# Batch 0's tails of k and v: issued by ScalarE ahead of its first table load instead of by GpSimd

## The chip, the cores and the metric

The kernel runs on one core of a Trainium2 chip. The metric is device time in microseconds (us) of one execution. Before the change the median of 3 runs is 270.94 us (270.31 to 272.93). The core's engines are TensorE (PE, with PEld for its weight loads), VectorE (DVE), ScalarE (ACT), GpSimd (POOL) and SyncE (SP). Each runs its own list of instructions in order, and issuing a DMA is one instruction of such a list.

## The reference

Two stages follow each other: an attention without softmax, and a feed-forward layer with a leaky ReLU.

```python
# q, k, v: (8 batches, 8 heads, 576 positions, 64)
def phi(x, c, s):
    r = np.maximum(x, 0.0)
    return np.concatenate([r * c, r * s], axis=-1)   # c, s: cos and sin of pi/2 * pos / 576
q_p, k_p = phi(q, cos_w, sin_w), phi(k, cos_w, sin_w)
kv  = np.einsum('bhsf,bhsd->bhfd', k_p, v)
z   = np.sum(k_p, axis=2)
num = np.einsum('bhsf,bhfd->bhsd', q_p, kv)
den = np.einsum('bhsf,bhf->bhs', q_p, z)[..., None] + 1e-06
attn = num / den                                     # -> x: (4608, 512)
h = x @ w_in                                         # (512, 2048)
out = np.maximum(0.01 * h, h) @ w_out                # (2048, 512)
```

## The kernel before

**Tiling.** The 576 positions of a batch are cut into a main part of 512 (four groups `j` of 128 partitions) and a tail of 64. Per batch, k and v give the 128x65 matrices `kv` of each head (64 columns of v and one of ones, which gives the denominator); q, scaled by cosine and sine and transposed, is multiplied with `kv` and divided into `xs` or `xp`; those rows, transposed again, are the right side of the first feed-forward product (`ps_h`, L460, L496, L782), whose leaky ReLU `g` enters the second (`ps_o`, L476, L883). Batches follow each other, and the tails of all q make a ninth group at the end. From batch 2 on a table of positions (`PLACE`, `AT`) sets the order; batches 0 and 1, which the change touches, are written out by hand, and the order is that of the code.

**The start, engine by engine.** SP issues, one behind the other, the two halves (heads 0 to 3, heads 4 to 7) of batch 0's q, then k's and v's first halves, k's and v's second halves (`load_main`, L93), and the eight pieces of the first weights (`load_w1`, L140). DVE clears a tile `blank`, with which TensorE runs 28 matmuls into an unused bank (`idle`, L168) until q is there. GpSimd makes the identity and the positions `pos` (L183 to L202), and then issues the four tail DMAs (`load_kvtail`, L103: k's tail and v's tail, each in two DMAs of 64 partitions by 4 heads by 64 numbers, so 256 bytes in one piece). ScalarE loads a table for the sine (L164), makes `cos_t` and `sin_t` (L216, L217) out of `pos`, and loads the table for ReLU and leaky ReLU (L218). Nothing of q, k or v can be scaled before `cos_t` and `sin_t` are made.

**Then batch 0.** DVE and ScalarE share the 16 scalings of q (`q_part`: half the heads, one group `j`, cosine or sine; groups 0 and 2 and the cosine of 3 are DVE's, group 1 and the sine of 3 are ScalarE's). TensorE transposes group by group (L366, `ps_qt`); each group needs both halves of the heads. ScalarE and DVE copy the results out (L247, L249). Then k's tail (`kpt`, DVE), k's first half (`kpm`), v's tail (`vtail`) and v's first half (`vmain`) are scaled or cast, behind 28 more blank matmuls (`kv_half(0, 0, "t", 14)`) TensorE makes the first half of `kv` (L290, L299, `ps_kvh`), and ScalarE casts it (L323). The second half of k follows on DVE and ScalarE, the second half of v is cast by GpSimd (L249). TensorE makes the numerators of the first half (L417, `ps_numh`), the second half of `kv`, the transposes `ps_xth` (L434) and the numerators of the second half, and goes over into the feed-forward layer of batch 0 (L460).

**DMA counters.** The DMAs that SP or ScalarE issues share eight completion counters in turn (`DMAHW0` to `DMAHW7`), and a ninth DMA waits until the first that used its counter has landed. GpSimd's have counters of their own (`DMASW`).

Of the kernel before, what the change touches and what calls it, by code (L numbers as in the profile page):

```python
# [18 lines left out]
def kernel(  # L19
# [14 lines left out]
    nc = tc.nc  # L34
# [49 lines left out]
    def staged(shape, name, soon=False):  # L84
        p, tag = (early, "early") if soon else (stage, "stage")
        return p.tile(shape, dt.float32, name=name, tag=tag)

    def load_main(nm, src, b, parts=(0, 1), soon=False):

        if parts[0] == 0:  # L90
            st[nm, b] = staged([P, H, J, D], f"{nm}st", soon)
        lo, hi = 4 * parts[0], 4 * parts[-1] + 4
        nc.sync.dma_start(  # L93
            st[nm, b][:, lo:hi],
            src[b, lo:hi, 0:MAIN, :].rearrange("h (p j) d -> p h j d", j=J),
        )

    def load_kvtail(nm, src, b, eng=nc.sync):

        t = kvtail.tile([P, H // 2, D], dt.float32, name=f"{nm}tl", tag="kvtail")  # L100
        v4 = src[b, :, MAIN:S, :].rearrange("(c o) p d -> o p c d", o=2)
        for o in range(2):
            eng.dma_start(t[o:P:2], v4[o])  # L103
        st[nm + "t", b] = t
# [41 lines left out]

    load_main("q", q, 0, (0,))
    load_main("q", q, 0, (1,))
    load_main("k", k, 0, (0,))
    load_main("v", v, 0, (0,))  # L150
    load_main("k", k, 0, (1,))
# [55 lines left out]
        allow_small_or_imprecise_dtypes=True,  # L207
    )
    sub_ = pos[:, J + 1 : J + 2]
    load_kvtail("k", k, 0, nc.gpsimd)  # L210
    load_kvtail("v", v, 0, nc.gpsimd)
    nc.vector.tensor_tensor(out=sub_, in0=sub_, in1=odd[:, 1:2], op=ALU.subtract)
    nc.vector.tensor_scalar(out=sub_, in0=sub_, scalar1=0.5, scalar2=None, op0=ALU.mult)
    cos_t = const.tile([P, J + 2], dt.float32, name="cos_t")
# [1189 lines left out]
```

## Time and profile before

| | |
|---|---|
| median of 3 runs | 270.94 us (270.31 to 272.93) |
| the profiled execution | 271.15 us, of which its span is 269.2 us |
| PE busy | 263.1 us, 98% of the span |
| DVE, ACT, POOL busy | 215.8, 203.9, 13.1 us |
| chain that ended last | PE 89%, DMA 5%, DVE 2% |
| tails of batch 0 | 4 DMAs of 64 KB, issued by POOL from 1.81 us to 4.42 us; 6.2 to 6.6 us to landing |

A row of the timeline or of the chain begins with its start and its length in us; the timeline's brackets hold the idle time of the engine before the row, and what ended it. Times in the text count from the start of the span.

### The profile page before, as it was taken

To read this page: it belongs to the slowest core of one execution; us is meant where nothing else is said; L and a number is where in the kernel's file an instruction comes from. 1 tells how busy PE (TensorE), PEld (TensorE's weight loads), DVE (VectorE), ACT (ScalarE), POOL (GpSimd) and SP (SyncE) were. 2 spreads that over 40 slices of the span, in tenths; PEclk is the share of its full clock that TensorE was granted. 3 is DMA by queue.
4 is the path that set the end of the run, shared out by engine and by line. 5 is a ranking of instruction groups with operands and counts; after the bars stand their busy time and mean duration, and the time that the engine had idled before them with its cause. 6 is when DMAs were issued, how large, how long until landed. Compare 5 with 4: busy or idle time off the path is not lost.

```text
span 269.2 us, 6819 instructions
## 1 busy us (share of the span) xinstructions
PE 263.1 (98%) x2742; PEld 230.1 (85%) x2742; DVE 215.8 (80%) x486; ACT 203.9 (76%) x347; POOL 13.1 (5%) x25
## 2 busy tenths in 40 slices
PE   8989999999999999999999999999999999999994
PEld 6976465666899989999999999999999999999983
DVE  5785798698997898897979797979789968966453
ACT  8756556695989998997798799888968757787621
POOL 5057001000000000000000000000000000000000
PEclk9999999999999999999999999999999999999999
DMA  6999999979999969999999799987267232200314
GB/s 221 380 394 413 394 367 376 366 140 285 285 248 285 193 206 245 360 168 256 270 238 140 247 280 185 173 243 162 65 102 178 45 74 67 111 2 0 156 41 117
DMA packets 86190, 57.05 MB, mean 212 GB/s; under 512 B 55632, under 2 KB 81232, under 8 KB 85648
## 3 DMA queue, kind: packets, MB, share of 16 engines
q1 hardware_dynamic: 85584, 55.98, 79.3%
q8 instruction: 21, 0.34, 0.5%
q10 hardware_dynamic: 448, 0.39, 0.4%
q0 software_dynamic: 128, 0.26, 0.3%
q14 instruction: 9, 0.07, 0.1%
HBM read 36.70 MB, written 9.44 MB: 171 GB/s over the span
## 4 chain that ended last, share of the span: by engine, by line
PE 89%; DMA 5%; DVE 2%; SPq 1%; issue 1%; POOL 0%; ACT 0%; DVEq 0%
PE ps_h L782 31%; PE ps_o L883 30%; PE ps_h L460 5%; PE ps_o L476 5%; PE ps_h L496 5%; DMA vst<-in_v_dram 4%; PE ps_num L381 3%; PE ps_h L883 3%; PE ps_o L973 2%; PE ps_kv L290 2%; DMA xT<-xs 1%; SPq L93 1%; PE ps_qt L366 1%; PE ps_numh L417 1%; PE ps_kvh L290 1%; PE ps_kv L299 1%
## 5 line engine op out<-in xcount | busy, mean ns | idle before, releaser
L883 PEld LDWEIGHTS <-g 128*128 128x128 f16 x584 | 56.3, 98 | 5.3
L782 PE MATMUL ps_h<-xT,w 128*128 128x256 f16 x336 | 49.0, 273 | 0.0
L782 PEld LDWEIGHTS <-w 128*128 128x128 f16 x448 | 47.9, 113 | 1.1 <-issue 0.2
L252 DVE TENSOR_TENSOR u<-ps_h,u 128x512 f32<-128x512 f32 x56 | 38.3, 685 | 10.2 <-PE ps_h L782 10.0
L883 PE MATMUL ps_o<-w,g 128*128 128x256 f16 x288 | 41.4, 273 | 0.0
L782 PEld LDWEIGHTS <-wa 128*128 128x128 f16 x336 | 36.0, 113 | 1.0 <-issue 0.4
L795 ACT ACTIVATE g<-ps_h 128x512 f16<-128x512 f32 x56 | 33.9, 605 | 3.7 <-PE ps_h L782 3.5
L802 ACT COPY u<-ps_h 128x512 f32<-128x512 f32 x56 | 32.7, 584 | 4.9 <-PE ps_h L782 4.8
L809 ACT ACTIVATE g<-u 128x1024 f16<-128x1024 f32 x28 | 29.7, 1062 | 8.4 <-DVE u L252 8.2
L782 PE MATMUL ps_h<-xw,wa 128*128 128x256 f16 x224 | 33.6, 273 | 0.0
L883 PE MATMUL ps_o<-wb,g 128*128 128x256 f16 x232 | 32.2, 273 | 0.0
L883 PEld LDWEIGHTS <-gs 128*128 128x128 f16 x256 | 24.9, 98 | 2.4
L901 ACT COPY ob<-ps_o 128x512 f32<-128x512 f32 (+1 forms) x32 | 18.1, 564 | 9.4 <-PE ps_o L883 9.1
L397 DVE TENSOR_TENSOR xs<-ps_num,rden 128x512 f16<-128x512 f32 x28 | 19.4, 691 | 1.0
L883 PE MATMUL ps_o<-w,gs 128*128 128x256 f16 x120 | 17.5, 273 | 0.0
L792 ACT COPY ps_h<-ps_h 128x512 f32<-128x512 f32 x28 | 16.0, 573 | 1.6 <-PE ps_h L782 0.7
L255 DVE TENSOR_TENSOR gs<-g 128x1024 f16<-128x1024 f16 x16 | 11.0, 685 | 7.8 <-ACT g L809 7.6
L782 PE MATMUL ps_h<-xT,wa 128*128 128x256 f16 x112 | 16.8, 273 | 0.2 <-DVE u L252 0.2
L883 PE MATMUL ps_o<-wb,gs 128*128 128x256 f16 x120 | 16.9, 273 | 0.0
L782 PE MATMUL ps_h<-xw,w 128*128 128x256 f16 x112 | 16.8, 273 | 0.0
L252 DVE TENSOR_TENSOR ob<-ps_o,ob 128x512 f32<-128x512 f32 (+1 forms) x22 | 14.7, 670 | 1.3 <-ACT ob L901 0.9
L496 PE MATMUL ps_h<-xT,w 128*128 128x512 f16 (+1 forms) x72 | 15.1, 355 | 0.0
(128 smaller groups left out, 435.6 us busy)
## 6 DMA issues: line engine op xcount, KB each, us to landing
qst<-in_q_dram SPq DMA_DIRECT2D x7, 1024.0 KB, 6.6
out_dram<-ob SPq DMA_DIRECT2D x14, 512.0 KB, 2.9
kst<-in_k_dram SPq DMA_DIRECT2D x6, 1024.0 KB, 7.9
vst<-in_v_dram SPq DMA_DIRECT2D x6, 1024.0 KB, 7.0
w1st<-in_moe_w_in_dram SPq DMA_DIRECT2D x8, 512.0 KB, 10.0
w2st<-in_moe_w_out_dram SPq DMA_DIRECT2D x4, 1024.0 KB, 12.3
kst<-in_k_dram SPq DMA_DIRECT2D x4, 512.0 KB, 8.4
vst<-in_v_dram SPq DMA_DIRECT2D x4, 512.0 KB, 8.9
```

What stands on the lines that cost most here:

```text
L252: nc.vector.tensor_tensor(out=o, in0=a, in1=b, op=ALU.add)
L397: nc.vector.tensor_tensor(out=xs, in0=ps[:, :, 0 : 4 * NE].rearrange("p a (b e) -> p a b e", e=NE)[:, :, :, 0:D], in1=rden.rearrange("p (a ...
L460: nc.tensor.matmul(ps[:, m % 2, lo:hi], lhsT=w1[m // 4][c // 2][:, c % 2, m % 4 : 512 : 4], rhs=xT[:, c, lo:hi], start=(c == 0 and lo == 0 ...
L476: nc.tensor.matmul(ps, lhsT=st["g", g][:, m, tt * P : (tt + 1) * P], rhs=w2[:, m, :], start=(m == 0), stop=(m == NFT - 1),)
L496: nc.tensor.matmul(ps[:, lo:hi], lhsT=w1[m // 4][c // 2][:, c % 2, m % 4 : 512 : 4], rhs=st["xT", g][:, c, lo:hi], start=(c == 0 and lo == 0),
L782: nc.tensor.matmul(bank[:, p], lhsT=w(c), rhs=st["xb", g][n][:, c], start=(fresh and p == 0 and c == 0), stop=(c == 1), skip_group_check=True,
L792: nc.scalar.copy(bank1[bj], bank1[bi])
L795: nc.scalar.activation(st["g" + nm, g][:, 2 * t : 2 * t + 2], bank1[bi], AF.Lrelu)
L802: nc.scalar.copy(st["u", g, t][:, n], bank1[bi])
L809: nc.scalar.activation(st["gt", g][:, :, 1, 2 * t : 2 * t + 2], st["u", g, t], AF.Lrelu)
L883: nc.tensor.matmul(bank[..., lo:hi], lhsT=st[G2[n], g][:, m, pair * P : (pair + 1) * P], rhs=W2[n](m)[:, lo:hi], start=(fresh and m == 0), ...
L901: nc.scalar.copy(o_at(g, half_, col, pair), bank_of(bi, pair, pair is None))
```

## The change

The two calls that load the tails of batch 0's k and v move up in the code, behind the two loads of q, and are given ScalarE as the issuing engine.

```diff
@@ -146,6 +146,8 @@
 
     load_main("q", q, 0, (0,))
     load_main("q", q, 0, (1,))
+    load_kvtail("k", k, 0, nc.scalar)
+    load_kvtail("v", v, 0, nc.scalar)
     load_main("k", k, 0, (0,))
     load_main("v", v, 0, (0,))
     load_main("k", k, 0, (1,))
@@ -207,8 +209,6 @@
         allow_small_or_imprecise_dtypes=True,
     )
     sub_ = pos[:, J + 1 : J + 2]
-    load_kvtail("k", k, 0, nc.gpsimd)
-    load_kvtail("v", v, 0, nc.gpsimd)
     nc.vector.tensor_tensor(out=sub_, in0=sub_, in1=odd[:, 1:2], op=ALU.subtract)
     nc.vector.tensor_scalar(out=sub_, in0=sub_, scalar1=0.5, scalar2=None, op0=ALU.mult)
     cos_t = const.tile([P, J + 2], dt.float32, name="cos_t")
```

The function that they call is the same:

```python
def load_kvtail(nm, src, b, eng=nc.sync):
    t = kvtail.tile([P, H // 2, D], dt.float32, name=f"{nm}tl", tag="kvtail")
    v4 = src[b, :, MAIN:S, :].rearrange("(c o) p d -> o p c d", o=2)
    for o in range(2):
        eng.dma_start(t[o:P:2], v4[o])
    st[nm + "t", b] = t
```

On ScalarE, at the very start of the program, this stands now (- before, + after; `ktl` and `vtl` are the tails, `warm` and `zero` one column each, whose only use is to have the table loaded):

```order
 L1399 UNCONDITIONAL_BRANCH
-L164 ACT_TABLE_LOAD
-L164 ACTIVATE warm<-zero 128x1
+L103 DMA ktl<-in_k_dram 64x4x64 x2
+L103 DMA vtl<-in_v_dram 64x4x64 x2
+L166 ACT_TABLE_LOAD
+L166 ACTIVATE warm<-zero 128x1
 L216 ACTIVATE cos_t<-pos,half_pi 128x6
 L217 ACTIVATE sin_t<-pos,zero 128x6
```

Four DMA issues stand ahead of the table load; the rest of ScalarE's list, and the lists of PE and DVE, keep their order. GpSimd's list is the same without its four issues.

On SP, at the start of its list, the DMAs are the same in the same order, with other waits. Before:

```order
L93 DMA qst_111<-in_q_dram 128x4x256 x2
L93 DMA kst_114<-in_k_dram 128x4x256
L93 DMA vst_116<-in_v_dram 128x4x256
L93 DMA kst_114<-in_k_dram 128x4x256
L93 DMA vst_116<-in_v_dram 128x4x256
L140 DMA w1st_120<-in_moe_w_in_dram 128x2x512 x2
```

After:

```order
L93 DMA qst_111<-in_q_dram 128x4x256 x2
L93 DMA kst_120<-in_k_dram 128x4x256
L93 DMA vst_122<-in_v_dram 128x4x256
L93 DMA kst_120<-in_k_dram 128x4x256 [waits DMAHW0_49]
L93 DMA vst_122<-in_v_dram 128x4x256 [waits DMAHW1_49]
L140 DMA w1st_126<-in_moe_w_in_dram 128x2x512 [waits DMAHW2_49]
```

The tails take four of the eight counters, so the second halves of k and v now wait for one DMA of k's tail (`DMAHW0`) and for q's first half (`DMAHW1`), and the first weights for the other DMA of k's tail (`DMAHW2`).

## The prediction

> **What bounds the kernel now.** I read the page first, then the chain of waits for the first 70 us, since the change touches only the start, and then the timeline of the first 20 us. The page puts 89% of the chain on PE. The chain of the start shows where that begins (start, length, what):
>
> ```profile
> 3.56 10.78 DMA vst<-in_v_dram
> 14.34 0.05 issue
> 14.39 1.18 POOL vmain L249 x2
> ...
> 16.18 0.39 ACT kv L323
> ...
> 19.84 12.11 PE ps_h L460 x64
> ```
>
> Until 14.34 us the kernel waits for the last piece of batch 0's v, GpSimd casts it, TensorE makes the second half of `kv`, ScalarE casts that at 16.18. From about 17 us TensorE works almost without a break; in the rows of the chain between there and 70 us the only other pieces are short steps of DVE that TensorE's own results start. So what the start gains or loses up to the cast at 16.18 reaches the end of the program undiminished: nothing later waits for a load.
>
> ScalarE's and DVE's first 16 us, from the timeline:
>
> ```profile
> 0.74 1.28 ACT L164 ACT_TABLE_LOAD   x1 [0.74 <-PEq L1388]
> 2.03 0.21 ACT L164 ACTIVATE warm<-zero 128x1 f16<-128x1 f32 x1
> 2.10 0.15 DVE L213 TENSOR_SCALAR pos<-pos 128x1 f32<-128x1 f32 x1
> 2.35 0.30 ACT L216 ACTIVATE cos_t<-pos,half_pi 128x6 f32<-128x6 f32 x1
> 2.86 1.28 ACT L218 ACT_TABLE_LOAD   x1
> 4.16 0.21 ACT L218 ACTIVATE warm<-zero 128x1 f16<-128x1 f32 x1
> 4.60 0.51 ACT L239 ACTIVATE qp<-qst,cos_t 128x256 f16<-128x256 f32 x1 [0.24 <-DMA qst<-in_q_dram]
> 4.61 0.35 DVE L241 TENSOR_SCALAR qp<-qst,cos_t 128x256 f16<-128x256 f32 x1 [1.78 <-DMA qst<-in_q_dram]
> 5.86 0.51 ACT L239 ACTIVATE qp<-qst,cos_t 128x256 f16<-128x256 f32 x1
> 6.27 0.89 ACT L239 ACTIVATE qp<-qst,sin_t 128x256 f16<-128x256 f32 x2
> 10.30 0.35 DVE L241 TENSOR_SCALAR kpm<-kst,cos_t 128x256 f16<-128x256 f32 x1
> 13.20 0.38 ACT L323 CAST kv<-ps_kvh 128x260 f16<-128x260 f32 x1 [0.62 <-PE ps_kvh L299]
> 13.88 0.89 ACT L239 ACTIVATE kpm<-kst,sin_t 128x256 f16<-128x256 f32 x2
> 14.32 0.16 DVE L392 TENSOR_SCALAR den<-ps_numh 128x8 f32<-128x8 f32 x1
> 15.86 0.69 DVE L397 TENSOR_TENSOR xp<-ps_numh,rden 128x512 f16<-128x512 f32 x1
> ```
>
> The reader is to see how little room ScalarE has. From its first instruction at 0.74 it loads, makes the tables' 12 columns, loads again, and is ready 0.24 us before q lands. DVE, by contrast, has 1.78 us of room there. ScalarE's last scaling of k ends at 13.88 + 0.89 = 14.77, only 0.8 us before GpSimd is done (14.39 + 1.18 = 15.57). TensorE in the same time:
>
> ```profile
> 1.09 6.11 PE L168 MATMUL ps_idle<-blank 128*128 128x256 f16 x28 [1.09 <-DVE blank L162]
> 7.70 0.61 PE L366 MATMUL ps_qt<-ident,qp 128*128 128x128 f16 x8
> 9.26 3.22 PE L168 MATMUL ps_kvh<-blank 128*128 128x256 f16 x28
> 12.35 0.69 PE L290 MATMUL ps_kvh<-vmain,kpm 128*128 128x65 f16 x16
> 12.89 0.28 PE L299 MATMUL ps_kvh<-vtail,kpt 128*128 128x130 f16 x2
> 13.63 0.67 PE L417 MATMUL ps_numh<-kv,qpT 128*128 128x65 f16 x16
> 16.86 0.38 PE L434 MATMUL ps_xth<-ident,xp 128*128 128x128 f16 x4
> ```
>
> **Taken off GpSimd.** Its four issues (1.81 to 4.42 us) go. Its next work waits for v:
>
> ```profile
> 3.19 1.23 POOL L103 DMA_DIRECT2D vtl<-in_v_dram  x2
> 14.39 1.17 POOL L249 CAST vmain<-vst 128x512 f16<-128x512 f32 x2 [9.97 <-DMA vst<-in_v_dram]
> ```
>
> With 9.97 us idle before the cast, this is worth nothing by itself.
>
> **Put on ScalarE.** Four issues now stand ahead of the first table load, in an engine that works in order. The trace has four issues of ScalarE, the stores at the end, and the chain has an issue of SP and the gap behind it:
>
> ```profile
> L917 ACTq DMA_DIRECT2D out_dram<-ob x4: 593/660/737, 262.9 to 265.8; - x4
> ```
> ```profile
> 0.73 0.47 SPq L93
> 1.21 0.06 issue
> ```
>
> I take the median: 4 x (0.66 + 0.05) = 2.84 us; with the ends, 2.57 to 3.15. Step by step:
>
> 1. The first table load moves from 0.74 to 3.58, its `warm` ends at 5.08. Before, the cosine waited for `pos` (2.10 + 0.15 = 2.25) about as long as for `warm` (2.24); so it now starts at 5.08 instead of 2.35, 2.73 later. The second load goes with it, and ScalarE is ready for q at 4.37 + 2.73 = 7.10 instead of starting at 4.60: **2.50 later**. DVE needs only the cosine and starts at about 5.4, 0.8 later; it is not the bound.
> 2. ScalarE's part of q's group 1 ends with the first of the two instructions at 6.27, at 6.78. TensorE transposes group 1 at 7.70, so 0.92 us of the delay is absorbed. 6.78 + 2.50 = 9.28, the transposes start at 9.31: **1.61 later**. The rest of the transposes, the copies, the 28 blank matmuls and ScalarE's k and v follow in the old order and stay 1.6 later: blanks at 10.87, `ps_kvh` at 13.96, the cast of `kv` at 14.81 instead of 13.20.
> 3. ScalarE's second half of k ends at 14.77 + 1.61 = 16.38, and is now later than GpSimd's cast, even if v lands no earlier. The 16 matmuls and the 2 of the tail take 12.89 - 12.35 + 0.28 = 0.82 us, nearly all behind that operand, so the second cast of `kv` starts at about 17.2 instead of 16.18: **1.0 later**.
> 4. DVE's divisions hang on the first numerators: `den` waits for half of the 13.63 row, so it moves from 14.32 to about 15.7, and the second `xp` from 15.86 to about 17.2, done at 17.9. TensorE transposes it at 17.93 instead of 16.86: **1.07 later**, the latest of the two paths. I take **+1.1 us**; 0.8 to 1.4 with the ends of the issue's cost.
>
> A cost below zero is excluded for the issues, since they take the sequencer's time; but the sum as a whole can fall below, which is a rival.
>
> **Moved on the DMA engines.** The tails now compete with q instead of k, and go through ScalarE's queue. What they cost before, and how many of batch 0's pieces were still moving after 12 us:
>
> ```profile
> q0 software_dynamic: 128, 0.26, 0.3%
> 4.00:5.00 1.00, 1.00 (x7) 0.70 (x5) 0.39 (x2) 0.75 (x3) 0.42 (x1) 1.00 1.09 387
> 5.00:6.00 1.00, 1.00 (x7) 0.69 (x6) 1.00 (x5) 1.00 (x4) 0.00 (x0) 1.00 1.00 305
> DMA packets 658, 1.21 MB, mean 402 GB/s; under 512 B 33, under 2 KB 118, under 8 KB 657
> ```
>
> (First row: queue, packets, MB, share; the next two end with the DMA share and GB/s of that microsecond; the last is 12 to 15 us.) The rate falls from 387 to 305 GB/s as the tails begin, and 118 - 33 = 85 pieces of 1 KB of q, k and v come after 12 us. On ScalarE's queue the tails would be 4 x 256 pieces of 256 B. Their cost lies between their bytes at 387 GB/s, 0.7 us, and 1,024 pieces at the mean price of a piece in the quiet row (4 to 5 us; 0.39 MB in 1 KB pieces is about 380 pieces a microsecond), 2.7 us. q's second half was there at 5.86; four pieces of 512 KB at 387 GB/s are 5.4 us more; so v's end lands between 12.0 and 14.0, against 14.34. GpSimd is then done by 15.2 at the latest, under the 16.38 of ScalarE: **0**, hidden by ScalarE's own delay with 1.2 us to spare. k's first half is asked for at 11.9 instead of 10.30; q's first half, even 0.7 late (5.3), is hidden by the cosine.
>
> SP's new waits: k's second half is issued when a tail of k has landed, v's when q's first half has (4.6 to 5.3, instead of 3.56). The DMA engines have q's second half, k's and v's first and k's second half queued, 4 x 1.35 us of work, so neither issue is missed: 0.
>
> **The rivals.**
>
> *Faster.* It may be that v's end was late because a few of the 16 engines fell behind while GpSimd's four DMAs ran; then it now lands near 12, GpSimd is done near 13.5, and the second cast waits for ScalarE alone. Were the issues free, that is 14.77 + 0.82 instead of 16.18, so -0.6 us: 270.3. It needs ScalarE's delay at q under 1.5 us (0.92 absorbed in step 2, 0.6 in step 3), that is issues of about 0.41 us and 0.05 between. For it speaks that SP's first issues took 0.47 in the chain; against it that none of ScalarE's four was under 0.593. The Trainium skill, "DMA: Bandwidth & Descriptors", section "Latency and other measured facts", says that two of the 16 DMA engines are usually slower and guesses at contention from GpSimd's descriptor rings; the late pieces agree, and the gain that it promises is this rival's. Chance 0.10.
>
> *No change.* Part of the four issues is hidden, or costs about 0.41 each: within 0.5 us of before, 270.9. The same page, section "Issuing engines are not separate DMA queues", says that the choice of the engine changes only the sequencer's time, usually small beside the transfer. By the page the sum would be near zero; the rows at 0.74 to 4.60, where ScalarE has 0.24 us of room, say that its sequencer's time is here the path. Chance 0.22.
>
> *Slower by more than 1%.* The issues are held up as SP's sixth was, when its queue was full:
>
> ```profile
> 3.56 1.78 SPq L93 DMA_DIRECT2D vst<-in_v_dram  x1
> ```
>
> If two of ScalarE's four take 1.78 instead of 0.66, ScalarE is 2.2 us later still, and the whole passes through: +3.3, 274.2. It decides from 1.6 us over the 2.84. Against it: the tails are small, have a queue of their own, and are issued before that sixth. Chance 0.06. In the same direction, TensorE may fall back in pace: the two rows of 28 blank matmuls show 218 ns each at the start and 115 ns later. Its pause between the transposes of groups 0 and 1 grows to some 1.3 us. If the blanks at 10.87 ran at the first pace, they would take 2.9 us more, +4.0 in all, 274.9. Before, no pause that long follows the faster pace, so the trace can't exclude it. The Trainium skill, "TensorE: Matmul & The Clock Gate", Part 1, has the clock fall only after an idle window of about 3.4 us; no run here shows that. Chance 0.02.
>
> **How the numbers follow.** The forecast (+0.8 to +1.4) has 0.60, the rivals 0.10, 0.22 and 0.08. The profiled execution took 271.15 us, 1.95 over its span of 269.2, and 0.2 over the median; the sum makes it 272.25, and 270.94 + 1.1 = 272.0 for the median. The three runs before spread by 2.6 us, so about 1% (2.7 us) is what can be told from no change. The range reaches down to the faster rival with 0.1 for a median's scatter (270.2), and up past the forecast's 1.4 by one held-up issue (1.1 us: 273.4); it leaves out the slower rivals and the tails. Faster by over 1% (under 268.2) no case gives: 0.02. Slower by over 1% (over 273.65) is the last rival: 0.08. Within 1%: 0.90.
>
> **What would show it.** Right: ScalarE's first table load at about 3.6 us, its first `qp` at about 7.1, the transposes at 7.70 now at 9.3, and in the chain, in place of v's landing and GpSimd's cast, ScalarE's steps from the issues to `kpm`; the cast of `kv` at about 17.2. Wrong: a table load before 2.5 us, v's landing still ending the wait before `ps_kvh`, TensorE's 28 blanks behind the transposes taking more than 3.3 us, or a time under 270.5 with ScalarE delayed as said, which would mean that something after 17 us takes the delay up.

## The result, and the profile after

The changed kernel takes 273.28 us (median of 12 runs, 272.04 to 274.12), the kernel before beside it 271.23 us (270.31 to 272.93): a ratio of 1.0074, with a 95% interval of 1.0053 to 1.0095, so 2.0 us more (1.4 to 2.6). The forecast was 272.0, within 270.2 to 273.4. The time lies in the range and within 1%, but the +1.1 us of the sum (0.8 to 1.4) is about half of what came. The profiled execution took 273.51 us, its span is 271.6.

ScalarE's start in the timeline of after (start, length, what; in brackets the idle time before it and what ended it):

```profile
0.73 1.45 ACTq L103 DMA_DIRECT2D ktl<-in_k_dram  x2
2.20 1.36 ACTq L103 DMA_DIRECT2D vtl<-in_v_dram  x2
3.60 1.28 ACT L166 ACT_TABLE_LOAD   x1 [3.60 <-issue]
5.00 0.29 ACT L216 ACTIVATE cos_t<-pos,half_pi 128x6 f32<-128x6 f32 x1
6.90 0.50 ACT L239 ACTIVATE qp<-qst,cos_t 128x256 f16<-128x256 f32 x1
14.35 0.38 ACT L323 CAST kv<-ps_kvh 128x260 f16<-128x260 f32 x1 [0.62 <-PE ps_kvh L299]
16.91 0.38 ACT L323 CAST kv<-ps_kvh 128x260 f16<-128x260 f32 x1 [0.98 <-PE ps_kvh L299]
```

The four issues take 2.81 us, the table load comes at 3.60 instead of 0.74, and the first scaling of q at 6.90 instead of 4.60. TensorE in the same time:

```profile
9.05 0.40 PE L366 MATMUL ps_qt<-ident,qp 128*128 128x128 f16 x4 [0.80 <-ACT qp L239]
10.40 3.22 PE L170 MATMUL ps_kvh<-blank 128*128 128x256 f16 x28
17.09 0.40 PE L434 MATMUL ps_xth<-ident,xp 128*128 128x128 f16 x4 [0.23 <-DVE xp L397]
18.20 0.40 PE L434 MATMUL ps_xth<-ident,xp 128*128 128x128 f16 x4 [0.45 <-DVE xp L397]
```

TensorE waits for ScalarE's `qp` and keeps the faster pace: 3.22 us for the 28 blank matmuls, as before. But the second transposes of `xp` come 1.34 us later than before's 16.86, and what they wait for is DVE. The chain of waits of after names the new piece:

```profile
0.73 4.14 DMA ktl<-in_k_dram
4.87 0.02 issue
4.89 5.84 DMA kst<-in_k_dram
10.72 0.03 issue
10.76 0.61 DVE kpt L241 x2
11.37 1.31 DVE kpm L241 x5
12.68 0.26 DVE vtail L224
12.94 0.34 DVE vmain L249
13.28 2.72 DVE kpm L241 x5
16.00 0.09 DVE den L392
```

It begins with k's tail and with k's second half, which SP may issue only behind it (4.89), and which lands at 10.72, just ahead of DVE's `kpt`. ScalarE's path is level with that one: in the second execution and in `e10_both` (both below) the chain begins with ScalarE's issues, and `kpt` stands at 10.80 and 10.77 instead of 10.76. What is new is the slow row of DVE. Five scalings of k in the first `kpm` row take 1.31 us, five of the same size in the second 2.72: four of them have gone from 0.35 us to 0.70. They run while GpSimd casts the second half of v, and then w1. The second five grouped by operation (smallest, median and largest duration in ns, first and last start), one row before and two after, and then GpSimd's casts after from the timeline:

```profile
L241 DVE TENSOR_SCALAR kpm<-kst,cos_t x3: 348/349/353, 13.0 to 14.1; 128x256 f16<-128x256 f32 x3
```

```profile
L241 DVE TENSOR_SCALAR kpm<-kst,cos_t x3: 335/693/705, 13.2 to 15.7; 128x256 f16<-128x256 f32 x3
L241 DVE TENSOR_SCALAR kpm<-kst,sin_t x2: 695/698/701, 13.8 to 15.0; 128x256 f16<-128x256 f32 x2
```

```profile
12.68 1.69 POOL L249 CAST vmain<-vst 128x512 f16<-128x512 f32 x2 [10.81 <-DMA vst<-in_v_dram]
14.31 1.28 POOL L249 CAST w<-w1st 128x512 f16<-128x512 f32 x2
```

Before, DVE's five stood from 13.0 to 14.4 and GpSimd began at 14.39; they did not meet. A second loss comes at 90 us. ScalarE waits there for batch 4's k, with TensorE's banks in its list behind that wait. Before, then after, then TensorE after:

```profile
87.80 0.72 ACT L239 ACTIVATE kpm<-kst,cos_t 128x512 f16<-128x512 f32 x1 [0.75 <-DMA kst<-in_k_dram]
```

```profile
90.30 0.72 ACT L239 ACTIVATE kpm<-kst,cos_t 128x512 f16<-128x512 f32 x1 [1.89 <-DMA kst<-in_k_dram]
```

```profile
92.04 0.60 PE L782 MATMUL ps_h<-xw,w 128*128 128x256 f16 x4 [0.46 <-ACT u L802]
93.48 0.60 PE L782 MATMUL ps_h<-xw,wa 128*128 128x256 f16 x4 [0.41 <-ACT ps_h L792]
```

TensorE, 1.36 us late until then, is 2.50 late behind these rows.

To compare the kernels below I take the start of the same matmul in each profiled execution, less its start in before's first one (us; the columns 17 to 114 are places by before's clock, and from 114 us to the end nothing moves by more than 0.01 us). Three more columns explain these: the end of TensorE's first 28 blank matmuls, and how long ScalarE waits at 90 us for batch 4's k and DVE at 112 us for batch 5's.

| | blanks end | 17 us | 87 us | 91 us | 110 us | 114 us | k at 90 | k at 112 |
|---|---|---|---|---|---|---|---|---|
| before | 7.20 | 0 | 0 | 0 | 0 | 0 | 0.75 | 0.66 |
| before, second execution | 7.23 | -0.44 | -0.42 | -0.25 | -0.25 | +0.19 | 0.93 | 1.14 |
| after | 6.47 | +1.35 | +1.36 | +2.50 | +2.48 | +2.71 | 1.89 | 0.94 |
| after, second execution | 6.19 | +1.86 | +1.87 | +2.86 | +2.92 | +3.17 | 1.74 | 0.96 |
| `e1_sp` | 6.82 | -0.73 | -0.72 | +0.61 | +0.62 | +0.62 | 2.09 | 0.51 |
| `e2_extra` | 6.26 | +0.65 | +0.66 | +2.34 | +2.50 | +3.78 | 2.43 | 1.99 |
| `e3_blanks` | 6.40 | +0.20 | +0.22 | +0.18 | +0.14 | +1.17 | 0.72 | 1.74 |
| `e4_late_v` | 6.51 | +0.70 | +0.71 | +1.25 | +1.44 | +1.75 | 1.30 | 1.01 |
| `e5_after_k4` | 6.51 | +1.41 | +1.43 | +1.37 | +1.70 | +1.70 | none | 0.66 |
| `e6_before_k4` | 6.83 | -0.85 | -0.83 | -0.89 | -0.51 | -0.41 | none | 0.80 |
| `e7_sp_k4` | 6.41 | -1.05 | -0.91 | -0.97 | -0.96 | -0.57 | none | 1.09 |
| `e8_half` | 6.60 | -0.73 | -0.71 | -0.77 | -1.09 | -0.37 | 0.32 | 1.43 |
| `e9_half_k4` | 7.24 | -0.44 | -0.42 | -0.48 | -0.37 | -0.24 | none | 0.84 |
| `e10_both` | 5.73 | +0.67 | +0.69 | +0.63 | +1.02 | +1.26 | none | 0.95 |

Two readings follow. Between 87 and 91 us TensorE loses what ScalarE's wait for k has over 0.75 us, and between 110 and 114 us what DVE's has over 0.71, to 0.02 us in each row that has such an excess; shorter waits are hidden. And the blanks' end is a second draw of the start. They begin at 1.08 to 1.09 in every execution, and their pace goes from 213 to 109 ns each at 4.0 us in `e10_both`, at 6.3 in `e6_before_k4`, and not before the last one in both executions of before and in `e9_half_k4`. Where v lands early and ScalarE holds nothing up, the second transposes of `xp` follow that end by 9.17 to 9.18 us (before's second execution, `e6_before_k4`, `e9_half_k4`).

### The profile page after: what moved, and what is told of

The parts are those of the page before. It is cut to its first block, busy times and chain, and to the rows that moved or that the text cites. A ratio compares the mean times of both kernels' runs of the same rounds, so it can differ in the third digit from the quotient of the medians.

```text
span 271.6 us, 6815 instructions
## 1 busy us (share of the span) xinstructions
PE 263.3 (97%) x2742; PEld 229.5 (85%) x2742; DVE 217.1 (80%) x486; ACT 203.9 (75%) x347; POOL 11.8 (4%) x21
## 4 chain that ended last, share of the span: by engine, by line
PE 85%; DMA 8%; DVE 4%; ACT 1%; issue 1%; SPq 0%; DVEq 0%; ACTq 0%
PE ps_o L883 29%; PE ps_h L782 28%; PE ps_h L460 5%; PE ps_o L476 5%; DMA kst<-in_k_dram 5%; PE ps_h L496 4%; PE ps_h L883 3%; PE ps_num L381 3%; PE ps_o L973 2%; PE ps_kv L290 2%; DMA ktl<-in_k_dram 2%; DVE kpm L241 2%; DMA xT<-xs 1%; DVE xp L397 1%; PE ps_qt L366 1%
## 5 line engine op out<-in xcount | busy, mean ns | idle before, releaser
L901 ACT COPY ob<-ps_o 128x512 f32<-128x512 f32 (+1 forms) x32 | 18.1, 565 | 9.3 <-PE ps_o L883 9.1
```

Of the source, the lines that this page charges most:

```text
L901: nc.scalar.copy(o_at(g, half_, col, pair), bank_of(bi, pair, pair is None))
```

## The experiments

Five explanations were to be told apart: A, ScalarE's late start alone; B, the tails' way through another queue; C, the meeting of DVE and GpSimd; D, that any later start grows along the program; E, ScalarE's wait for batch 4's k at 90 us. Medians are of 12 runs where nothing else is said, ratios are to the kernel before on the same chip. The experiments ran on three chips, so times of different experiments are compared by their ratios (0.001 is 0.27 us); each ratio is uncertain by some 0.6 us, and a difference of two by some 0.8.

**The tails issued by SP.** Against the changed kernel; k's tail goes behind k's first half, v's behind v's:

```diff
-    load_kvtail("k", k, 0, nc.scalar)
-    load_kvtail("v", v, 0, nc.scalar)
     load_main("k", k, 0, (0,))
+    load_kvtail("k", k, 0)
     load_main("v", v, 0, (0,))
+    load_kvtail("v", v, 0)
```

> Batch 0's tails are issued by SP, k's behind k's first half and v's behind v's first half; neither GpSimd nor ScalarE issues a load. Theory A (the time comes from ScalarE's late start): ScalarE's first table load is back at 0.74 us, its first scaling of q at about 4.6, v's last piece lands near 12.7 as in the changed kernel, and the time is that of the kernel before or up to 0.6 us less (270.6 to 271.3). Theory B (the time comes from the way of the tails: 256-byte pieces in a hardware queue, and SP's waits on shared counters): 272.5 to 273.3, with ScalarE on time. Theory C (GpSimd's cast of v, now earlier, and DVE's scalings of k slow each other): the five scalings of k's second half take over 2 us instead of 1.3 and eat the gain, 271.2 to 271.8.

Measured: 270.74 us (269.63 to 271.98), ratio 0.9985 (0.9958 to 1.0012). ScalarE is on time, DVE's five scalings take 0.35 us each, the start is 0.73 ahead; v's last piece, expected near 12.7, landed at 13.6. Through SP's queue the tails cost nothing, so B falls, and A stands. At 90 us it loses 1.33 although its start is early: that loss does not need a late start.

**ScalarE delayed, the tails left where they were.** Against the kernel before: GpSimd loads the tails, and ScalarE issues four loads of 16-byte pieces that nothing reads.

```diff
+    for nm, src in (("k", k), ("v", v)):
+        spare = const.tile([P, H // 2, 4], dt.float32, name=f"{nm}spare")
+        v4 = src[0, :, MAIN:S, :].rearrange("(c o) p d -> o p c d", o=2)
+        for o in range(2):
+            nc.scalar.dma_start(spare[o:P:2], v4[o][:, :, 0:4])
```

> The kernel before, with four extra loads of the same form (64 partitions by 4 heads, but only 16 bytes in a piece, into tiles that nothing reads) issued by ScalarE ahead of its first table load; GpSimd issues the tails as before. Theory A: the table load moves to about 3.6 us, ScalarE's first scaling of q to about 6.9, the second cast of kv to about 17, and the time is 272.2 to 273.3. Theory B: within 0.4 us of before (271.2). Theory C: DVE's five scalings of k's second half mostly keep 0.27 us each, since v lands late (about 14.3) as before, so the time is up to 0.4 us under that of the changed kernel (273.3).

Measured: 274.1 us (273.69 to 274.73, 6 runs), ratio 1.0123 (1.009 to 1.0156). ScalarE's rows are those of after:

```profile
3.60 1.28 ACT L169 ACT_TABLE_LOAD   x1 [3.60 <-issue]
6.89 0.49 ACT L244 ACTIVATE qp<-qst,cos_t 128x256 f16<-128x256 f32 x1
14.17 1.44 POOL L254 CAST vmain<-vst 128x512 f16<-128x512 f32 x2 [9.74 <-DMA vst<-in_v_dram]
```

The kernel is slower without the tails on ScalarE, and by more than the 272.2 to 273.3 that A gave. The extra loads take the same counters as in the change, so SP issues k's second half late here, too (4.88); but so it does in `e8_half` below (4.90), which loses nothing, and that leaves ScalarE's delay. Here v landed late (GpSimd's cast at 14.17), DVE's five kept 0.35 us, and the start lost 0.65. It grew by 1.7 at 90 us and by 1.3 at 117 us of its own clock, where TensorE waits 1.12 us for DVE's `xs`, as the waits for k say (2.43 and 1.99 us); what part the extra loads have in k's late landings stays open.

**TensorE delayed, ScalarE left alone.** Against the kernel before, 12 more blank matmuls ahead of the first half of `kv`:

```diff
-    kv_half(0, 0, "t", 14)
+    kv_half(0, 0, "t", 20)
```

> The kernel before with 12 more blank matmuls of 109 ns ahead of the first half of kv (40 instead of 28), so that TensorE comes 1.3 us late into the feed-forward layer and every load and every issue stays as before. Theory D (any delay of 1.3 us at the start grows to 2 us, because the loads behind 60 us meet other traffic): 273.0 to 273.4, with the growth at 85 to 95 us of the trace. If the growth belongs to the changed loads alone: 272.3 to 272.7, a plain shift by 1.3 us.

Measured: 274.08 us (272.42 to 274.63, 6 runs), ratio 1.0107 (1.007 to 1.0144). The 40 blanks take 4.53 us against 3.22, so 1.3 are put in and 2.9 come out, more than the 273.0 to 273.4 that D gave. The profiled execution, the fastest of the six, doesn't bear D out: TensorE's first blanks ended 0.8 us early in it and v landed at 14.5, its second transposes of `xp` are only 0.21 late, and yet it loses 1.0 at 112 us, where DVE waits 1.74 us for k, and nothing at 90 us. With `e1_sp`, which loses 1.33 from an early start, this says that the losses go with k's landings and not with the lateness. Where the other five executions lose their time, no trace shows.

**The meeting taken away.** Against the changed kernel, the second half of v is issued behind the first piece of w1, so that it lands later:

```diff
     load_main("k", k, 0, (1,))
+    load_w1(0, 0)
     load_main("v", v, 0, (1,))
     for i in range(NB):
-        for cp in range(2):
+        for cp in range(i == 0, 2):
```

> The changed kernel with the second half of v issued behind the first piece of the weights, so that it lands some 1.3 us later (near 14.0) and GpSimd's cast falls behind DVE's scalings of k's second half. Theory C: those five scalings take about 1.4 us in all instead of 2.7, the second group of transposes of x (18.20 in the changed kernel) comes 0.4 to 0.7 us earlier, and the time is 272.6 to 272.9. Without C: 273.3 or, if the cast is now the last, up to 273.8.

Measured: 272.55 us (271.56 to 273.43), ratio 1.0059 (1.0032 to 1.0086). A row each of DVE, GpSimd and TensorE:

```profile
13.76 0.34 DVE L242 TENSOR_SCALAR kpm<-kst,cos_t 128x256 f16<-128x256 f32 x1
13.99 1.66 POOL L250 CAST vmain<-vst 128x512 f16<-128x512 f32 x2 [12.12 <-DMA vst<-in_v_dram]
17.55 0.40 PE L435 MATMUL ps_xth<-ident,xp 128*128 128x128 f16 x4
```

v lands 1.3 us later, and the second transposes of `xp` come 0.65 us *earlier* than in after (17.55 against 18.20), since all five scalings are back at 0.35. That is C, shown in the trace: 0.65 us. In the times it is 0.4 us by the ratios (1.0074 and 1.0059), less than their uncertainty.

**ScalarE's wait at 90 us moved.** One number of the table of positions, in the changed kernel (`e5_after_k4`), in the kernel before (`e6_before_k4`) and in the kernel with the tails on SP (`e7_sp_k4`): ScalarE's scaling of batch 4's first piece of k, key (4, 0, 0).

```diff
-            81.995, (4, 0, 1): 89.4, (4, 1, 1): 103.9, (4, 4, 0): 111.3, (5, 2, 0): 139.6, (5, 3, 0):
+            91.4, (4, 0, 1): 89.4, (4, 1, 1): 103.9, (4, 4, 0): 111.3, (5, 2, 0): 139.6, (5, 3, 0):
```

> The changed kernel with one scaling of batch 4's k on ScalarE (head group 0, cosine) four instructions further back, behind the copies of the feed-forward layer that stood behind it. Theory E (the growth at 90 us is ScalarE, which waits in order for batch 4's k and holds up TensorE's banks): TensorE's two waits at 92.0 and 93.5 us go or fall under 0.4 us together, and the time is 272.1 to 272.6. Rival (the growth is spread over the later loads, or is scatter): 273.0 to 273.6.

> The kernel before with the same one scaling moved back. Theory E: in the profiled execution before, ScalarE waited 0.75 us there and TensorE did not, so it is a slack that is just used up: 270.4 to 271.2, the same or a few tenths less. Rival: no difference at all, or slower because the scaling now stands in the way of the next.

> SP issues batch 0's tails (k's behind k's first half, v's behind v's first half), and the same one scaling of batch 4's k is moved back. With the tails on SP the start was 0.73 us earlier and lost 1.3 us again at 90 us. Theory E: that loss goes, 269.8 to 270.3, under the kernel before. Rival: 270.5 to 271.2, as without the move.

Measured: 272.95 us (272.53 to 273.75), ratio 1.0058 (1.0033 to 1.0082); 270.92 (270.51 to 271.99), 0.9981 (0.9959 to 1.0004); 270.29 (269.54 to 271.94), 0.9966 (0.9939 to 0.9994). In all three the growth at 90 us is gone (table above, 87 to 91 us: -0.06 each), so E has the place right. By the ratios it gave 0.4 us in the changed kernel, where 0.7 to 1.2 was expected; 0.3 was lost again at 97 us, and the profiled execution was the fastest of its kernel.

`e6_before_k4` showed something that was not asked: its start is that of the kernel before, instruction for instruction, and was 0.85 us ahead of it. Of this 0.44 goes with v's early landing (12.6), as in before's second execution below, and 0.41 with the first blanks, which ended at 6.83 instead of 7.23 there.

**One tail on ScalarE, one on SP.** Against the changed kernel, ScalarE issues the two DMAs of k's tail, and SP those of v's:

```diff
     load_kvtail("k", k, 0, nc.scalar)
-    load_kvtail("v", v, 0, nc.scalar)
     load_main("k", k, 0, (0,))
     load_main("v", v, 0, (0,))
+    load_kvtail("v", v, 0)
```

> Half of the change: ScalarE issues the two DMAs of k's tail ahead of its table load, SP those of v's tail behind v's first half; GpSimd issues none. Theory A with the slack of 0.92 us in front of the transposes of q's group 1: ScalarE is 1.4 us late at its table load and about 1.1 at q's first scaling, 0.2 of which is left at the transposes; TensorE reaches the feed-forward layer 0.4 to 0.7 us earlier than before, and the time is that with the tails on SP (270.5 to 271.1). Rival (ScalarE's delay passes through in proportion): about half of the change's 2 us, 271.8 to 272.3.

Measured: 269.98 us (269.51 to 271.23), ratio 0.9954 (0.993 to 0.9978), faster than both kernels.

```profile
2.22 1.28 ACT L166 ACT_TABLE_LOAD   x1 [2.22 <-issue]
5.52 0.49 ACT L239 ACTIVATE qp<-qst,cos_t 128x256 f16<-128x256 f32 x1
12.70 1.52 POOL L249 CAST vmain<-vst 128x512 f16<-128x512 f32 x2 [10.83 <-DMA vst<-in_v_dram]
16.12 0.40 PE L434 MATMUL ps_xth<-ident,xp 128*128 128x128 f16 x4
```

ScalarE is 0.92 us late at q (5.52 against 4.60), and the second transposes of `xp` are early, in part because the first blanks ended at 6.60 here. The like comparison is `e9_half_k4` below, which has the same start, with before's second execution: the blanks end at 7.24 and 7.23, and the second transposes of `xp` stand at 16.41 in both. So the room that TensorE leaves ScalarE's group 1 is there: two issues cost nothing, four cost. A loss in proportion to the issues is refuted. The room is not the same in each execution, though, since TensorE's blanks set it: in `e3_blanks`, where they ended at 6.40, group 1's transposes start at 7.04, only 0.25 us behind ScalarE.

**The same with the wait at 90 us moved**, by the number above:

> The kernel of e8_half (ScalarE issues k's tail alone, SP issues v's tail behind v's first half) with ScalarE's scaling of batch 4's first piece of k moved from place 81.995 to 91.4. Theory (a later start and ScalarE's wait for batch 4's k at 90 us are two separate losses, and both are taken away here): start about 0.7 us ahead of before's profiled execution, no growth at 90 us, so 269.6 to 270.2 us, level with or 0.1 to 0.4 under the 269.98 of e8_half. Rival (the move matters only where the start is late; here k lands in time anyway): the same as e8_half, 269.8 to 270.2. Rival (moving the scaling costs something of its own): over 270.4.

Measured: 270.29 us (269.99 to 271.02), ratio 0.9975 (0.9949 to 1.0001), nothing gained. Its start is 0.44 ahead and not 0.7, with the blanks at their slow pace to the end. In `e8_half` k lands in time there, with 0.32 us of waiting, so nothing was to be had.

**Second executions**, of the changed kernel and of the kernel before, unaltered:

> The changed kernel once more, unaltered, for a second profiled execution. Theory (the start's delay belongs to the change, since ScalarE's four issues and GpSimd's cast beside DVE's scalings are in its order): ScalarE's first table load at 3.60 within 0.05, v's end at 12.4 to 12.9, DVE's five scalings of k 0.6 to 0.7 us each, the x transposes at 18.1 to 18.3. Rival (the doubled scalings were one execution's accident): 0.35 us each, x transposes at about 17.6. The growth behind 60 us is expected to come again at 90 us (0.8 to 1.5), its size not the same.

> The kernel before once more, unaltered, for another profiled execution. Theory (the late pieces of v behind GpSimd's descriptors differ between executions): v's end lands anywhere from 12.6 to 14.5 us, and the x transposes stand between 16.0 and 16.9 with it; if it lands near 12.6 the span is 0.4 to 1.0 us under the 269.2 of the first. Rival (v's end is at 14.3 in every execution of this kernel, and the early landing belonged to the moved scaling): 14.2 to 14.5.

Measured: 274.08 and 271.34 us, one run each. The chain of waits of the second execution of after:

```profile
0.73 0.74 ACTq L103
...
7.04 2.00 ACT qp L239 x5
...
9.09 0.41 PE ps_qt L366 x4
...
13.32 3.20 DVE kpm L241 x5
...
18.71 0.40 PE ps_xth L434 x4
```

This is the chain that the prediction asked for, from ScalarE's issues over `qp` to TensorE, with DVE's slowed `kpm` behind it (3.20 us for the five; the transposes are later than the 18.1 to 18.3 expected). And before, in its second execution, GpSimd, DVE and TensorE:

```profile
12.79 1.72 POOL L249 CAST vmain<-vst 128x512 f16<-128x512 f32 x2 [8.36 <-DMA vst<-in_v_dram]
```

```profile
12.61 0.35 DVE L241 TENSOR_SCALAR kpm<-kst,cos_t 128x256 f16<-128x256 f32 x1
12.87 0.35 DVE L241 TENSOR_SCALAR kpm<-kst,sin_t 128x256 f16<-128x256 f32 x1
```

```profile
16.41 0.40 PE L434 MATMUL ps_xth<-ident,xp 128*128 128x128 f16 x4
```

v was there at 12.7, without the change. So the landing at 14.34, with which the prediction's chain began, belonged to that execution. DVE is already at its third scaling when GpSimd begins, and keeps 0.35 us. The span, expected 0.4 to 1.0 us under the first, was 269.4 against 269.2: the 0.44 ahead at 17 us was lost again at 90 and 112 us, where ScalarE and DVE waited 0.93 and 1.14 us for k.

**Both repairs in the changed kernel**, `e4_late_v` with the number above:

> The changed kernel with both repairs: v's second half issued behind the first piece of w1 (so GpSimd's cast comes when DVE's five scalings are nearly done) and ScalarE's scaling of batch 4's first piece of k moved from place 81.995 to 91.4. Theory (the loss is ScalarE's late start, about 1.1 us against a start whose v lands at 12.7, plus the collision, plus the wait at 90 us): the first part alone is left, x transposes at 17.5 to 17.6, no growth at 90 us, so 0.9 to 1.4 us over before: 271.9 to 272.4. Rival (the two repairs overlap, or the loss has another source): no better than the better of the two alone, 272.5 or more. Rival (the growth at 90 us follows from any change of the start and comes back elsewhere): over 272.9.

Measured: 271.92 us (271.02 to 272.6), ratio 1.0017 (0.9994 to 1.004). The second transposes of `xp` stand at 17.52, 1.11 us behind before's second execution, and nothing grows at 90 us. By the ratios the repairs gave 0.4 us each alone, and 1.5 together. Against `e6_before_k4`, which has the same move at 90 us, 1.0 us is left (1.0017 and 0.9981). The two differ in the tails' way and in v's place, too; the chain of waits of `e10_both` names ScalarE, and from the blanks at 10.57 to the feed-forward layer it stays with TensorE but for the cast of `kv`:

```profile
0.73 0.74 ACTq L103
...
7.02 2.00 ACT qp L240 x5
...
10.57 3.06 PE ps_kvh L171 x28
```

So this 1.0 us is ScalarE's late start.

## Why the prediction was half right

- **ScalarE's issues and its late start: right.** Four issues and their gaps were put at 2.84 us and took 2.87 (0.73 to 3.60); the table load was put at 3.58, the cosine at 5.08 (5.00), the first `qp` at 7.10 (6.90). `e2_extra` shows that the delay costs time without the tails, `e8_half` and `e9_half_k4` that 0.92 us of it is absorbed.
- **What of it reaches the first cast of `kv`: too large by 0.46.** It was put at 14.81 and came at 14.35. 0.2 of that is the earlier `qp`; and the transposes of group 1 were taken as one block of eight that waits, though its first four ran ahead, at 7.85, so that only four stood behind ScalarE (9.05).
- **"0, hidden", for GpSimd's earlier end: this term failed.** GpSimd's cast was weighed only by when it ends. What counts is when it runs: DVE's five scalings, 1.1 us later than before, now fall into it and take 0.70 instead of 0.35. `den` was put at 15.7 and would have come at 15.2 (`e4_late_v`: 15.26); it came at 15.92. By the trace of `e4_late_v` the term is 0.65 us, in the second execution of after 1.16 (18.71 against 17.55).
- **The base of the sum was one execution's.** Step 3 and step 4 were counted from a start whose v landed at 14.34, and step 2 from transposes (7.70) that stood there because the first blanks ran at their slow pace to the end. In the executions of the same start that I have, v landed at 14.34, 12.74 (second execution), 12.61 (`e6_before_k4`) and 14.54 (`e3_blanks`), and the blanks ended at 7.20, 7.23, 6.83 and 6.40; in the second and third TensorE stood 0.44 and 0.85 us earlier. The +1.07 of step 4 is what `e10_both` shows against the second execution (1.11), but partly by luck: a late base and a too large delay of ScalarE's offset each other. Against the start of `e6_before_k4` it is 1.52.
- **A row misread.** The fall from 387 to 305 GB/s between 4 and 6 us was put down to the tails. Only 1 of their 128 packets is in the row of 5 to 6 us; in the second execution, where none is, the rate is 305 as well. The sum doesn't use it beyond the bounds of v's landing (12.0 to 14.0; it came at 12.62).
- **"Nothing later waits for a load" failed.** It was read from the chain up to 70 us. At 90 us ScalarE waits for batch 4's k before and after, for 0.75 us where TensorE doesn't feel it, and for 1.89 us where it loses 1.14. `e5_after_k4` takes that away. But `e1_sp` loses 1.33 there with an early start: it is not simply the start's delay that grows, it is when k lands. SP issues that load at 81.25 before, 83.04 after and 81.06 in `e1_sp`, and ScalarE starts 6.5, 7.3 and 7.3 us later. At 112 us DVE waits for batch 5's k in the same way. What sets these landings from execution to execution was not settled.
- **The rivals.** The faster one had v's landing right (12.62), but ScalarE was late by more than the 1.5 us it allowed. No issue was held up as SP's sixth, and TensorE's pace held over a pause of 0.80 us in front of group 1's transposes, so both slower rivals fell. TensorE's pause was put at 1.3 us. That SP's queue was full in that sixth issue is the prediction's reading; the row shows its 1.78 us. "No change" fell as well: the four issues took 0.65 to 0.72 us each, not 0.41.
- **The sum in times.** By the ratios 1.5 us goes from the changed kernel to `e10_both`, with the meeting and the wait at 90 us; 1.0 from there to `e6_before_k4`, with ScalarE's late start; and `e6_before_k4` is 0.5 under the kernel before. That 1.5 + 1.0 - 0.5 gives the 2.0 of the result is no test, since each step begins where the one before it ends, and each of the first two is uncertain by some 0.8 us. So the term that was put at +1.1 measured 1.0 in the times and 1.1 to 1.5 in the traces, and as much again came from two terms that were put at nothing. How these two share it the times can't tell; in the traces the meeting is 0.65 to 1.16 us and the wait at 90 us about 1.0 to 1.1.

## What to carry to other kernels

Count the issues that are put on an engine as time of that engine, and lay them against the room that its first consumer leaves: here 0.92 us in the profile that the sum was taken from, good for two issues and not for four. When a start moves, look also at what it moves *into*: two engines that never met before may then run at the same time. A landing time that one profile shows is one draw, and so is the time at which TensorE's pace changes; where a sum starts from either, take a second execution first. A wait that costs nothing in the profile may be close to costing: here all that came on top of 0.75 and 0.71 us was lost in full.

## What the runs showed of the hardware

DVE's scalings (128x256, float32 to float16) and GpSimd's casts (128x512, the same types) disturb each other, and in two ways. Where GpSimd's cast asked while the third or a later one of DVE's five ran (`e2_extra`, `e4_late_v`, `e6_before_k4`, `e8_half`, `e9_half_k4`, `e10_both`, before's second execution), DVE kept 0.35 us each, and GpSimd's first cast took 0.79 to 1.16 us instead of 0.61, longest where most of DVE's series was still to come. Where it asked before the second (both executions of after, and `e5_after_k4`), the two took turns: in after DVE's instructions start at 13.19, 13.81, 14.43 and 15.05, and GpSimd's at 13.69, 14.31 and 14.93, both 0.62 us apart. The Trainium skill, "SBUF — State Buffer", section "Who interferes with whom", says that DVE and GpSimd share a pair of ports as an exclusive lock, which DVE needs in its two-port modes, and which is held for a whole instruction while the other fully blocks. That the two take turns agrees with it; that each is kept out for the whole of the other's instruction these runs don't show, since a turn of 0.62 us is less than the 0.26 and 0.56 us that the two take alone from start to start, added up. That a series of DVE's instructions keeps GpSimd out over three or four of them is not said there, and why one case goes the one way and one the other, these runs don't show.

Batch 0's last piece of v landed between 12.6 and 14.5 us in the executions in which GpSimd issued the tails, and between 12.6 and 13.6 in those in which it did not and v's place was kept. The same program gave 14.34 and 12.74.

TensorE's pace doubled after a time that was not the same in each execution. The first blank matmuls began at 1.08 to 1.09 us in all fourteen; the step from 213 to 109 ns each came at 4.0 us at the earliest, and in three executions not before the 28th had ended at 7.2. Later blanks kept the faster pace over a pause of 0.80 us (28 in 3.22 us).
